# Loading the ninth query block of batch 0 behind the weights, and turning it between the first matmuls

## The chip, the cores and the metric

The kernel runs on one core of a Trainium2 chip. The metric is device time in microseconds (us) of one execution; the median over several executions is quoted. Positions inside an execution are from the profile and count from the start of the profiled span. Engines: PE is TensorE (matmuls), PEld its weight loads, DVE is VectorE, ACT is ScalarE, POOL is GpSimd.

## The reference, cut to what matters

```python
# q, k, v: (8 batches, 8 heads, 576, 64)
def phi(x, c, s):
    r = np.maximum(x, 0.0)
    return np.concatenate([r * c, r * s], axis=-1)      # c, s: cos and sin of the position
q_p, k_p = phi(q, cos_w, sin_w), phi(k, cos_w, sin_w)
kv  = einsum('bhsf,bhsd->bhfd', k_p, v)
num = einsum('bhsf,bhfd->bhsd', q_p, kv)
den = einsum('bhsf,bhf->bhs', q_p, k_p.sum(axis=2))[..., None] + 1e-06
attn = num / den
x = attn.transpose(0, 2, 1, 3).reshape(4608, 512)
h = x @ w_in                                            # 512 x 2048
g = h * (1.0 / (1.0 + np.exp(-beta * h)))
out = g @ w_out                                         # 2048 x 512
```

The linear attention is small beside the two matrix products. The kernel walks over x in chunks of 512 rows (8 blocks of 64). A batch has 576 rows, which are 9 blocks, so the ninth block of batch 0 is wanted only by chunk 1.

## The kernel before

The load of the inputs of one batch, and the order in which batch 0 starts:

```python
def load_raw(b, name, j0=0, j1=4):
    js = slice(j0, j1)
    src = {"q": q, "k": k, "v": v}[name][b]
    nc.sync.dma_start(
        out=raw_tile(b, name)[:, js].rearrange("q j n d -> q j (n d)"),
        in_=src.rearrange("(j g) (p n) d -> (g p) j (n d)", g=2, n=NQ)[:, js, :])
# ... cut ...
load_raw(0, "q", 0, 2)
load_raw(0, "q", 2, 4)
# ... cut: beta ...
load_raw(0, "v", 0, 2)
load_raw(0, "k", 0, 2)
load_raw(0, "v", 2, 4)        # what the start waits for
load_raw(0, "k", 2, 3)
load_raw(0, "k", 3, 4)
load_w("in", 0, 2)
# ... cut: later w_in 1, 2 and 3 ...
```

x is needed turned (features on partitions). Eight of the nine blocks of batch 0 are turned by TensorE, the ninth by a DMA that transposes. `q_relu` makes qb from the raw q, `q_turn_pe` turns qb into qt (and qs, its product with a tangent), `num_mm` multiplies these by kv, `x_rden` and `x_mul` divide. From here on TensorE works through slots: in chunk 0, slots 4 to 15 are four matmuls of h each, slots 16 to 31 four of the output each. What else is to be done hangs between slots:

```python
def rest():                                   # in slot 4
    cast_halves(2)                            # w_in 2 and 3 to bf16, mostly on VectorE
    cast_halves(3)
    x_mul(x_rden(2, 0, 8, NQ, (0, 1)), 8, NQ) # ninth block
    # ... cut: loads of w_out and of batch 1 ...
    x_turn_dma(0, 8, 9)                       # ninth block turned by a DMA
    for j in range(8):
        cast_out(j)                           # w_out to bf16, on VectorE
    v_scale(1, 0); k_relu(1); q_relu(1, 0); q_relu(1, 1)

early = {
    4: lambda: (num_mm(8, 0, 2, 0), num_mm(8, 1, 2, 1), rest()),
    15: lambda: v_scale(1, 1, eng="act"),
    22: lambda: (kv_mm(1, 0, 6), kv_mm(1, 1, 6), kv_take((0, 1), 6, "act")),
    23: second,                               # queries of batch 1 turned on TensorE
    25: lambda: (num_seven(0, 4), ...),       # 7 x 8 products of batch 1
    26: lambda: (num_seven(1, 6), ...),       # 7 x 8 more
    # ... cut ...
}
# in slot 24: load_raw(2, name) for q, v, k of batch 2
```

`warm_pe(n, w)` and `warm_long(n)` are matmuls whose results nobody uses; they fill TensorE's idle time at the start.

## Time and profile before

| | before |
|---|---|
| three runs | 294.04 to 295.37 us, median 294.3 |
| profiled span | 292.4 us |
| TensorE busy | 284.0 us (97%) |
| half of v lands | 12.40 us |
| VectorE's 20 casts of w_in end | 29.48 us |
| matmuls of kv of batch 1 begin | 38.08 us |
| first h of chunk 1 begins | 50.69 us |

How to read it: TensorE is the bound, so a change is worth what it moves TensorE's work.

### The profile page before, as it was taken

To read this page: it belongs to the slowest core of one execution; us is meant where nothing else is said; L and a number is where in the kernel's file an instruction comes from. 1 tells how busy PE (TensorE), PEld (TensorE's weight loads), DVE (VectorE), ACT (ScalarE), POOL (GpSimd) and SP (SyncE) were. 2 spreads that over 40 slices of the span, in tenths; PEclk is the share of its full clock that TensorE was granted. 3 is DMA by queue.
4 is the path that set the end of the run, shared out by engine and by line. 5 is a ranking of instruction groups with operands and counts; after the bars stand their busy time and mean duration, and the time that the engine had idled before them with its cause. 6 is when DMAs were issued, how large, how long until landed. Compare 5 with 4: busy or idle time off the path is not lost.

```text
span 292.4 us, 7218 instructions
## 1 busy us (share of the span) xinstructions
PE 284.0 (97%) x3072; PEld 141.3 (48%) x3072; DVE 114.0 (39%) x287; ACT 142.8 (49%) x228; POOL 74.9 (26%) x89
## 2 busy tenths in 40 slices
PE   7699999999999999999999999999999999999994
PEld 6354455455445544554445444454455444444444
DVE  5889975834900392029301950086005000000000
ACT  5778856862166315721573137412760277137511
POOL 1444000643380038202650265023601210000000
PEclk9999999999999999999999999999999999999999
DMA  6999999999998089907991699139102810131033
GB/s 242 383 389 385 392 349 334 299 264 336 176 284 314 3 159 203 402 34 141 216 392 46 130 217 391 58 65 206 36 2 52 143 36 0 39 83 23 0 74 72
DMA packets 50737, 53.89 MB, mean 184 GB/s; under 512 B 31233, under 2 KB 31633, under 8 KB 50705
## 3 DMA queue, kind: packets, MB, share of 16 engines
q1 hardware_dynamic: 47744, 45.95, 53.8%
q0 software_dynamic: 2688, 7.34, 10.5%
q8 instruction: 24, 0.39, 0.5%
q10 hardware_dynamic: 272, 0.14, 0.2%
q14 instruction: 9, 0.07, 0.1%
HBM read 36.71 MB, written 9.44 MB: 158 GB/s over the span
## 4 chain that ended last, share of the span: by engine, by line
PE 92%; DMA 3%; DVE 2%; SPq 1%; issue 1%
PE ps L365 42%; PE ps L390 42%; PE ps L280 3%; DMA raw_v<-in_v_dram 3%; PE ps L259 3%; PE ps L408 1%; SPq L78 1%; DVE xs L302 1%; PE ps L229 0%; PE ps L339 0%; DVE win L108 0%; DVE rden L295 0%; DVE den L291 0%; DVE rk L189 0%; DVE vb L204 0%
## 5 line engine op out<-in xcount | busy, mean ns | idle before, releaser
L365 PE MATMUL ps<-xt,win 128*128 128x512 bf16 (+1 forms) x580 | 127.3, 378 | 0.1
L390 PE MATMUL ps<-wout,g_t 128*128 128x512 bf16 x560 | 124.4, 379 | 0.0
L372 ACT ACTIVATE g_t<-ps,beta 128x512 bf16<-128x512 f32 x144 | 98.6, 688 | 33.2 <-PE ps L365 33.2
L365 PEld LDWEIGHTS <-win 128*128 128x128 bf16 x580 | 56.0, 98 | 66.0 <-issue 0.5
L390 PEld LDWEIGHTS <-g_t 128*128 128x128 bf16 x560 | 53.7, 98 | 63.9 <-issue 0.3
L385 POOL DMA_DIRECT2D out_dram<-o_sb x56 | 35.9, 645 | 136.7 <-ACT o_sb L396 136.7
L396 ACT COPY o_sb<-ps 128x512 f32<-128x512 f32 x35 | 20.2, 588 | 98.2 <-PE ps L390 94.0
L271 DVE CAST kv<-ps 128x520 bf16<-128x520 f32 x6 | 4.2, 700 | 68.3 <-PE ps L259 68.3
L217 POOL TENSOR_TENSOR qs<-qt,tanr 128x1152 bf16<-128x1152 bf16 x12 | 28.3, 2382 | 8.2 <-DMA qt<-qb 8.2
L411 DVE COPY o_sb<-ps 128x256 f32<-128x256 f32 (+1 forms) x2 | 0.7, 358 | 62.7 <-PE ps L408 62.7
L302 DVE TENSOR_TENSOR xs<-ps,rden 128x768 bf16<-128x768 f32 (+4 forms) x26 | 22.8, 884 | 0.9 <-DVE rden L295 0.2
L291 DVE TENSOR_TENSOR den<-ps,eps 128x12 f32<-128x12 f32 (+4 forms) x26 | 4.1, 159 | 33.6 <-PE ps L280 33.5
L214 DVE TENSOR_SCALAR vb<-raw_v,cos 128x256 bf16<-128x256 f32 x63 | 17.1, 347 | 0.0
L214 DVE TENSOR_SCALAR vb<-raw_v,sin 128x256 bf16<-128x256 f32 x54 | 14.7, 349 | 0.0
L280 PEld LDWEIGHTS <-qt 64*64 64x64 bf16 x576 | 10.4, 106 | 4.9 <-issue 4.5
L259 PE MATMUL ps<-vb,rk 64*64 64x130 bf16 x576 | 10.2, 218 | 2.1 <-ACT rk L187 1.9
L280 PE MATMUL ps<-kv,qt 64*64 64x65 bf16 x576 | 11.7, 195 | 0.5 <-ACT kv L269 0.5
L189 DVE TENSOR_SCALAR qb<-raw_q 128x1152 bf16<-128x1152 f32 x16 | 11.4, 752 | 1.6 <-DMA raw_q<-in_q_dram 1.6
L259 PEld LDWEIGHTS <-rk 64*64 64x64 bf16 x576 | 8.5, 106 | 6.9 <-ACT rk L187 3.6
L280 PE MATMUL ps<-kv,qs 64*64 64x65 bf16 x576 | 11.5, 193 | 0.0
L108 DVE CAST win<-w_stage 64x512 bf16<-64x512 f32 x22 | 10.9, 493 | 1.1 <-DMA w_stage<-in_moe_w_in_dram 0.6
L189 DVE TENSOR_SCALAR rk<-raw_k 128x2304 bf16<-128x2304 f32 (+2 forms) x9 | 10.7, 1186 | 0.6 <-DMA raw_k<-in_k_dram 0.6
(59 smaller groups left out, 98.6 us busy)
## 6 DMA issues: line engine op xcount, KB each, us to landing
raw_v<-in_v_dram SPq DMA_DIRECT2D x7, 1152.0 KB, 10.4
raw_k<-in_k_dram SPq DMA_DIRECT2D x7, 1152.0 KB, 13.6
raw_q<-in_q_dram SPq DMA_DIRECT2D x7, 1152.0 KB, 7.3
out_dram<-o_sb POOLq DMA_DIRECT2D x56, 128.0 KB, 4.4
w_stage<-in_moe_w_in_dram SPq DMA_DIRECT2D x3, 1024.0 KB, 13.4
w_stage<-in_moe_w_out_dram SPq DMA_DIRECT2D x2, 1024.0 KB, 8.0
w_stage<-in_moe_w_out_dram SPq DMA_DIRECT2D x4, 512.0 KB, 12.0
out_dram<-o_sb SPq DMA_DIRECT2D x14, 128.0 KB, 2.3
```

Source lines behind the costliest of these rows:

```text
L108: nc.vector.tensor_copy(o, a)
L189: nc.vector.tensor_scalar(dst, src, scalar1=0.0, scalar2=None, op0=ALU.max)
L214: nc.vector.tensor_scalar(o, a, scalar1=t[:, n : n + 1], scalar2=None, op0=ALU.mult)
L217: eng.tensor_tensor(dst.rearrange("q n (g p) -> q n g p", g=2), src.rearrange("q n (g p) -> q n g p", g=2), tanr[:, n0:n1].unsqueeze(2).to ...
L259: nc.tensor.matmul(t[jj * HP : (jj + 1) * HP, g], lhsT=rk[hs, n, 2 * jp + jj, :], rhs=vb[hs, n, 2 * jp + jj].rearrange("q s e -> q (s e)") ...
L280: nc.tensor.matmul(ps[cols, bank + jj, slot * E : (slot + 1) * E], lhsT=(qt, qs)[cs][rows, jp, n, cols], rhs=kv[rows, g, jp, cs, :], start ...
L302: nc.vector.tensor_tensor(o.rearrange("q j n s d -> q j (n s) d"), nv[:, :, a:z, :, 0:D].rearrange("q j n s d -> q j (n s) d"), rden[:, :, ...
L365: nc.tensor.matmul(ps[:, h_bank(c, jt), blocks.start * 64 : blocks.stop * 64], lhsT=win[jt // 4][:, mi, (jt % 4) * P : (jt % 4 + 1) * P], ...
L372: nc.scalar.activation(g_t, ps[:, h_bank(c, jt)], AF.Silu, scale=beta[:, jt : jt + 1])
L385: eng.dma_start(out=out_v[bb, n][:, m0:m1], in_=o_sb[hf * HP : (hf + 1) * HP, m0:m1])
L390: nc.tensor.matmul(o_ps, lhsT=gs[c, jt][:, tt * P : (tt + 1) * P], rhs=wout[jt // 4][:, jt % 4, :], start=(jt == 0), stop=(jt == JT - 1))
L396: nc.scalar.copy(o_sb, o_ps)
```

## The change

The intent: 131 KB less ahead of the loads that the start waits for. The ninth block of batch 0's queries is not wanted before chunk 1, so it is loaded behind w_in 3, and its relu, its turn, its products and its division move from the start to later slots.

```diff
-    load_raw(0, "q", 0, 2)
-    load_raw(0, "q", 2, 4)
+    load_raw(0, "q", 0, 2, 0, 8)          # load_raw takes blocks n0 to n1 now
+    load_raw(0, "q", 2, 4, 0, 8)
...
-    q_relu(0, 0)                          # and likewise q_relu(0, 1)
+    q_relu(0, 0, n1=8)
-    warm_pe(9, 48, bank=2)
-    q_turn_pe(0, 0, 4)                    # and likewise q_turn_pe(0, 1, ...)
+    warm_pe(11, 48, bank=2)
+    q_turn_pe(0, 0, 4, end=8)
...
     for i in range(1, 4):
         load_w("in", i)
+    load_raw(0, "q", 0, 4, 8, NQ)
...
+    def q_turn_eight(bank):               # two transposes on TensorE
+        t = ps[:, bank].bitcast(BF16)[:, 0 : 2 * P].rearrange("q (s c) -> q s c", c=P)
+        for jp in range(2):
+            nc.tensor.matmul(t[:, jp], lhsT=qb[:, jp, 8, :], rhs=ident,
+                             is_transpose=True, start=(jp == 0), stop=(jp == 1))
+        nc.scalar.copy(qt[:, :, 8], t)
+        for jp in range(2):
+            tan_mul(nc.vector, qs[:, jp, 8:NQ], t[:, jp].unsqueeze(1), 8, NQ)
...
     def rest():
         cast_halves(2)
         cast_halves(3)
-        x_mul(x_rden(2, 0, 8, NQ, (0, 1)), 8, NQ)
+        q_relu(0, 0, n0=8)
+        q_relu(0, 1, n0=8)
...
+    def eight():
+        for jp in range(2):
+            num_mm(8, jp, 2, jp)
+        x_mul(x_rden(2, 0, 8, NQ, (0, 1)), 8, NQ)
         x_turn_dma(0, 8, 9)
         for j in range(8):
             cast_out(j)
...
     early = {
-        4: lambda: (num_mm(8, 0, 2, 0), num_mm(8, 1, 2, 1), rest()),
+        4: rest,
+        11: lambda: q_turn_eight(1),
+        13: eight,
```

More of the change, by code (lines that the diff above doesn't have):

```diff
@@ L73, in raw_tile, with load_raw @@
         return raws[name, b]
-    def load_raw(b, name, j0=0, j1=4):
+    def load_raw(b, name, j0=0, j1=4, n0=0, n1=NQ):
         js = slice(j0, j1)
@@ L78, in load_raw @@
         nc.sync.dma_start(
-            out=raw_tile(b, name)[:, js].rearrange("q j n d -> q j (n d)"),
-            in_=src.rearrange("(j g) (p n) d -> (g p) j (n d)", g=2, n=NQ)[:, js, :])
+            out=raw_tile(b, name)[:, js, n0:n1].rearrange("q j n d -> q j (n d)"),
+            in_=src.rearrange("(j g) (p n) d -> (g p) j (n d)", g=2, n=NQ)[:, js, n0 * D : n1 * D])
     win = [const.tile([P, MI, 512], BF16, name=f"win{i}") for i in range(4)]
@@ L189, in relu, with q_relu @@
             nc.vector.tensor_scalar(dst, src, scalar1=0.0, scalar2=None, op0=ALU.max)
-    def q_relu(b, jp, eng="dve"):
-        relu(qb[:, jp].rearrange("q n (j d) -> q j n d", j=2), raw_tile(b, "q")[:, 2 * jp : 2 * jp + 2], eng)
+    def q_relu(b, jp, eng="dve", n0=0, n1=NQ):
+        relu(qb[:, jp, n0:n1].rearrange("q n (j d) -> q j n d", j=2),
+             raw_tile(b, "q")[:, 2 * jp : 2 * jp + 2, n0:n1], eng)
     def k_relu(b, j0=0, j1=4, eng="dve", n0=0, n1=NQ):
@@ L219, in tan_mul, with q_turn_pe @@
             tanr[:, n0:n1].unsqueeze(2).to_broadcast([P, n1 - n0, 2, HP]), op=ALU.mult)
-    def q_turn_pe(b, jp, bank, hold=False):
-        parts = ((0, 0, 5), (1, 5, NQ))
+    def q_turn_pe(b, jp, bank, hold=False, end=NQ):
+        parts = ((0, 0, 5), (1, 5, end))
         v2 = []
@@ L440 @@
     nc.vector.tensor_copy(ps[:, 0, 16 : 16 + NQ], sin9)
-    q_relu(0, 1)
+    q_relu(0, 1, n1=8)
     warm_pe(6, 128, bank=2)
-    warm_pe(9, 48, bank=2)
-    q_turn_pe(0, 0, 4)
+    warm_pe(11, 48, bank=2)
+    q_turn_pe(0, 0, 4, end=8)
     nc.vector.reciprocal(rbeta, beta)
     warm_pe(1)
-    take = q_turn_pe(0, 1, 2, hold=True)
+    take = q_turn_pe(0, 1, 2, hold=True, end=8)
     warm_long(2)
```

## The prediction

> **What bounds the kernel now.** I read the page first (busy shares, then the chain that ended last), then the chain in order of time for the first 60 us, then the timelines of PE, DVE, ACT, POOL and of the load queue for the first 55 us, and last the busy time in stretches. From the page:
>
> ```profile
> PE 284.0 (97%) x3072; PEld 141.3 (48%) x3072; DVE 114.0 (39%) x287; ACT 142.8 (49%) x228; POOL 74.9 (26%) x89
> PE 92%; DMA 3%; DVE 2%; SPq 1%; issue 1%
> ```
>
> TensorE is the bound: 92% of the chain is its work. The stretches show where it is not (columns: stretch, its length, then busy time and count of each engine, granted clock, DMA share, GB/s):
>
> ```profile
> 9.00:12.40 3.40, 1.53 (x83) 1.00 (x84) 2.64 (x3) 2.00 (x4) 1.63 (x1) 1.00 1.04 400
> 12.40:15.00 2.60, 1.85 (x63) 0.85 (x54) 2.50 (x7) 2.56 (x8) 1.26 (x1) 1.00 1.03 390
> 22.50:32.00 9.50, 9.50 (x46) 4.27 (x46) 9.10 (x21) 7.71 (x12) 2.50 (x4) 1.00 1.05 387
> 32.00:52.00 20.00, 19.97 (x318) 10.54 (x317) 14.01 (x30) 13.24 (x26) 1.02 (x2) 1.00 1.06 355
> ```
>
> From about 19 us to the end TensorE has no gap (9.50 of 9.50, 19.97 of 20.00; stretches from 52 to 280 us read 100% too). So only two things move the time: how early the gapless stretch begins, and whether something opens a gap in it. The start is set by loads; the chain in order of time (start, length, what) begins so:
>
> ```profile
> 3.06 9.34 DMA raw_v<-in_v_dram
> 12.42 0.35 DVE vb L204
> 14.74 1.06 DVE xs L302 x2
> 17.71 1.06 DVE xs L302 x2
> 18.82 0.40 PE ps L339 x4
> 19.22 3.03 PE ps L365 x18
> 22.25 0.25 PE ps L280 x16
> 22.50 9.60 PE ps L365 x44
> ```
>
> The second half of batch 0's v lands at 12.4 us; DVE, idle for 0.78 us before it, then works through to 18.77, and TensorE turns the last quarter of x and is dense from there. The last two lines matter for the gap: 0.25 us of the ninth block's products (slot 4), then 44 matmuls, four each for slots 5 to 15, 0.863 us a slot. DVE in the same time (start, length, instruction, idle before it):
>
> ```profile
> 19.33 10.16 DVE L108 CAST win<-w_stage 64x512 bf16<-64x512 f32 x20 [0.56 <-DMA w_stage<-in_moe_w_in_dram]
> 29.52 0.16 DVE L291 TENSOR_TENSOR den<-ps,eps 128x4 f32<-128x4 f32 x1
> 29.71 0.18 DVE L295 RECIPROCAL rden<-den 128x4 f32<-128x4 f32 x1
> 29.93 0.42 DVE L302 TENSOR_TENSOR xs<-ps,rden 128x256 bf16<-128x256 f32 x1
> 30.27 3.25 DVE L116 TENSOR_SCALAR wout<-w_stage,rbeta 128x512 bf16<-128x512 f32 x8
> 33.45 2.46 DVE L214 TENSOR_SCALAR vb<-raw_v,cos 128x256 bf16<-128x256 f32 x9
> 36.47 1.36 DVE L189 TENSOR_SCALAR rk<-raw_k 128x2304 bf16<-128x2304 f32 x1 [0.56 <-DMA raw_k<-in_k_dram]
> ```
>
> DVE casts w_in 1, 2 and 3 without a break from 19.33 to 29.48. Put beside TensorE's slots, this queue is only just ahead: the last cast for slot 12 (w_in 3, first half) ends near 28.15 and slot 12 begins at 22.44 + 7 x 0.863 = 28.48. That is the line the change touches.
>
> [...] The trace agrees on DVE: its rows stand in program order. [...] The trace agrees: the casts have median 422 ns and maximum 768, the long ones where POOL casts too (22.0 to 23.6 and 24.7 to 26.1 us). So the 20 casts take 10.16 us, not 20 x 0.44. [...] The new transfer has rows of 256 B; no load of before has such rows, so its price is not shown. [...] Before has idle of 1.40 us ahead of its first kv matmuls with a granted clock of 1.00.
>
> **The change, part by part.**
>
> Loads: the two q transfers shrink from 9 to 8 blocks: 128 x 4 x 256 B = 131 KB less ahead of everything that the start waits for. At 385 to 400 GB/s that is 0.34 us. v, k and w_in all land 0.34 earlier.
>
> Start, DVE and ACT: two relus, two tan products and two copies lose a ninth or a quarter of their width, two transposes leave, and two 48-wide warm matmuls come in to fill the place. DVE was idle 0.78 us before the v load, so this alone is worth nothing; it only makes sure DVE is ready for the earlier load. From there everything is a chain of DVE work and loads, so dense matmuls begin 0.34 earlier, at about 18.7 instead of 19.06. The casts of w_in 1 also wait for their load (0.56 us of idle), so they go from 18.99 to 29.14.
>
> Slot 4: the 16 small matmuls (0.25 us) go to slot 13; no work saved, but slot 5 now starts 0.34 + 0.25 = 0.59 earlier.
>
> Slot 11: two transposes, 0.05 us each of TensorE time, and they need qb of block 8. In DVE's order the two relus of it stand behind all 20 casts. One of them is 128 wide: from 1152 wide at 0.752 us and 2304 wide at 1.361, 0.53 ns per element, so 0.752 - 1024 x 0.00053 = 0.21 us; two back to back overlap by some 0.07, 0.35 together. They end at 29.18 + 0.35 = 29.53. TensorE has finished slot 11 at 28.48 - 0.59 = 27.89. It waits until about 29.42 for the first and 29.57 for the second: a new gap of 1.5 us. Slot 12 begins at about 29.65, against 28.48 before: 1.17 later, in spite of the earlier start. Both sides of this subtraction are on clocks that I have, so I trust it more than any other number here.
>
> Slot 13: ACT's copy and DVE's two tan products follow the transposes and end near 30.5, and slot 13 ends at 29.65 + 1.73 = 31.38, so its products don't wait; they cost the 0.25 that slot 4 gave up. TensorE is 1.42 late.
>
> w_out casts: they now stand behind the sums and division of slot 13. Products end at 31.63, sum, reciprocal and product take the 0.75 that they took before (29.52 to 30.27), so the casts start at 32.4 instead of 30.27, one each 0.406. The fourth is done at 34.1. Slot 16 starts at 31.94 + 1.42 = 33.36 and wants the fourth 0.65 later, at 34.0: some 0.1 us of wait. TensorE is now 1.5 late.
>
> Behind that: DVE ends these casts at 35.65, v at 38.1, relu of k at 39.45. The kv matmuls of batch 1 came at 38.08 and now at 39.6, so they just clear it. Nothing later has slack to give back.
>
> Sum: -0.34 (start) - 0.25 (slot 4 emptied) + 1.5 (gap) + 0.1 (transposes, nearly all of it after the gap) + 0.25 (slot 13) + 0.1 (first w_out casts) = about +1.4 to +1.5 us. 294.3 + 1.5 = 295.8.
>
> **Rivals.** A, no gap: the relus of block 8 come in time, and only the load counts: 294.3 - 0.34 + 0.1 = 294.0. For it: the slots look chosen with care, and the load lands in time. On the last point I estimate: w_in 3 is down at 24.7 in before (POOL waits for it until then), so at 24.4 now, and 131 KB at even half rate takes 0.7 us, so 25.1. Against it: the load is not the last thing waited for, the cast queue is, and its end at 29.48 stands in the profile; for no gap the casts would have to be 1.5 us faster. I give it 1 in 8. B, the gap also costs clock: [...] Against: idle of 1.40 us at 1.00. 1 in 25. C, the late DVE queue opens a second gap at the kv matmuls of batch 1: my margin there is 0.15 us, and the k load itself moves to 36.5 or 36.9 at its slow rate, still well ahead of the relu at 38.1. It would add 0.1 to 0.4: 296.1. 1 in 4. D, the narrower q gains more at the start than its bytes, because DVE and ACT there get shorter: up to 0.3 more, 295.5. The gap's far end moves with the casts' load, so such a gain survives only as far as w_in 1 lands earlier.
>
> **Range and chances.** The centre is the subtraction at slot 12 plus what follows, 295.8. The low end 294.7 holds a gap half as long as I think, the high end 296.6 rival C with some chip-to-chip spread (three runs of before span 1.3 us). A change of 2% would be 5.9 us, four times my effect: faster 0.005, same 0.985, slower 0.01.
>
> **What would show it.** The v load ends near 12.05 and TensorE's dense stretch starts near 18.7: the 0.34. DVE's row of 20 casts ends near 29.15, with two 128-wide relus behind it. TensorE's timeline shows two transposes near 29.5 with about 1.5 us of idle ahead of them, released by DVE's qb: if no idle stands there, the prediction is wrong. PE busy in 22.5 to 32 us falls from 9.50 to about 8. The w_out casts start near 32.4, slot 16 near 33.4, kv matmuls near 39.6. Granted clock stays at 1.00 behind the gap. What would make it wrong: casts that run faster than before, or a start that moves by much more than 0.34.

This is what the traces show. In before the rows of VectorE stand in program order (20 casts from 19.33 to 29.48 us, the sum at 29.52, the reciprocal at 29.71), and in after the two relus behind the same 20 casts began at 28.80, 0.03 us after the last cast's end. Of before's 20 casts, 16 took 418 to 424 ns and four 723 to 768, and those four overlapped GpSimd's casts (22.02 to 23.64 and 24.71 to 26.08 us).

## More of the kernel before

Instead of busy shares it is best to take landmarks, events on TensorE that both kernels have, and to compare their times; where the difference between the kernels jumps from one landmark to the next, something happened between them.

Chain of waits in order of time (start, length, what):

```profile
40.29 1.34 PE ps L229 x18
41.64 1.73 PE ps L390 x8
44.91 0.58 PE ps L280 x53
```

The 18 transposes of batch 1's queries took 1.34 us here, and after the change 1.00. The products of slot 26 (53 of the 56 in this line) follow without a gap.

## The result, and the profile after

| | before | after |
|---|---|---|
| fast runs | 6, median 294.44 us | 6, median 297.12 us (296.86 to 297.87) |
| ratio of the fast runs | | 1.009 (95%: 1.0068 to 1.0113) |
| profiled span | 292.4 us | 295.5 us |

All ratios here are the mean time of one kernel's fast runs over the mean time of the other's fast runs of the same rounds, so they are not quite the ratios of the medians. The change makes the kernel 2.7 us slower. That is within 2%, but above the range on record.

The page of the kernel after: busy times, then q8, the queue of kind "instruction" that has the most packets (packets, MB, share of 16 engines), then the chain that ended last.

```profile
PE 284.2 (96%) x3049; PEld 143.2 (48%) x3074; DVE 114.5 (39%) x291; ACT 142.6 (48%) x229; POOL 75.7 (26%) x89
q8 instruction: 24, 0.39, 0.5%
PE 88%; DVE 5%; DMA 3%; issue 2%; SPq 1%
```

TensorE's work is the same; its chain has lost 4 points, to DVE and to "issue", which is time in which an engine waits for nothing that the profile shows. The stretches, columns as in the prediction, say where (two of after, then the second one of before):

```profile
22.50:32.00 9.50, 8.70 (x56) 3.82 (x55) 7.32 (x20) 7.28 (x12) 2.00 (x3) 1.00 1.06 381
40.00:52.00 12.00, 10.20 (x220) 6.26 (x212) 8.00 (x16) 6.92 (x11) 0.00 (x0) 1.00 1.06 347
40.00:52.00 12.00, 11.97 (x215) 6.58 (x214) 8.22 (x16) 8.57 (x16) 1.02 (x2) 1.00 1.06 332
```

The first stretch lost 0.80 us of TensorE, which was foreseen in kind. The second lost 1.80 us (before was busy for 11.97 of those 12.00), which was not. VectorE's timeline shows the first cause (start, length, instruction, idle before it):

```profile
18.71 10.06 DVE L108 CAST win<-w_stage 64x512 bf16<-64x512 f32 x20
28.80 0.36 DVE L189 TENSOR_SCALAR qb<-raw_q 128x128 bf16<-128x128 f32 x2
32.23 3.25 DVE L116 TENSOR_SCALAR wout<-w_stage,rbeta 128x512 bf16<-128x512 f32 x8
```

The two relus do stand behind all 20 casts. TensorE's chain in order of time, at that place and at the second one:

```profile
29.08 0.36 PE ps L247 x2
29.45 1.73 PE ps L375 x8
...
45.89 0.15 PE ps L290 x4
46.05 1.54 issue
47.59 0.61 PE ps L290 x52
```

At 29.08 the two transposes begin, after 0.81 us of idle that DVE's qb ended. At 46.05, four products into the 56 of slot 26, TensorE stops for 1.54 us. No other engine, no semaphore and no data is named for it.

The landmarks on TensorE, from both timelines and chains:

| landmark | before | after | difference |
|---|---|---|---|
| dense h matmuls begin | 19.06 | 19.04 | -0.02 |
| slot 12 | 28.48 | 29.28 | +0.80 |
| slot 16 | 31.94 | 33.09 | +1.15 |
| kv matmuls of batch 1 | 38.08 | 39.43 | +1.35 |
| slot 24, behind the turned queries of batch 1 | 41.64 | 42.62 | +0.98 |
| first h of chunk 1 | 50.69 | 53.40 | +2.71 |
| first h of chunk 5 | 172.55 | 175.26 | +2.71 |

So two things make up the 2.7 us: about 1.0 us up to slot 24, and 1.54 us in the gap at 46.05. The small rest, 0.19 us, lies in pieces of a few hundredths. From chunk 1 to chunk 5 nothing more is lost. Near 194 us the chain of after has another 0.60 us of "issue", and this profiled execution has a total 0.4 us above what the medians differ by. It is not peculiar to after: TensorE's weight loads stand idle for 0.3 to 0.8 us at this place in 14 of the 20 profiles, in before's too (0.34 us, without a hole in its chain). It comes up again below.

**Why the earlier load gave nothing.** The second half of v lands at 11.98 instead of 12.40 us, and VectorE starts its next work earlier by as much. Two casts of w_in 0 then take it back. VectorE in before, then in after:

```profile
15.83 1.18 DVE L108 CAST win<-w_stage 64x512 bf16<-64x512 f32 x2
17.04 0.17 DVE L291 TENSOR_TENSOR den<-ps,eps 128x14 f32<-128x14 f32 x1
```

```profile
15.42 1.57 DVE L108 CAST win<-w_stage 64x512 bf16<-64x512 f32 x2
17.02 0.17 DVE L301 TENSOR_TENSOR den<-ps,eps 128x14 f32<-128x14 f32 x1
```

The pair starts 0.41 us earlier and takes 0.39 us longer (0.82 and 0.72 us each, against 0.42 and 0.72 in before). GpSimd casts other parts of w_in 0 at the same time: it starts them at 14.69 in after and at 15.30 in before, while VectorE starts at 15.42 and 15.83. That fits the long casts of before that the prediction reads (723 to 768 ns against 418 to 424, all four overlapping GpSimd's); the size of it is what the prediction lacked. Overlap alone does not make a cast long: the one at 15.83 in before took 0.42 us although GpSimd was casting (15.30 to 15.91 and 15.97 to 16.73). This is an argument from the two timelines, and the one experiment on it, below, did not settle it.

**What the second gap could be.** The page of after has on q8, of kind "instruction", 24 packets, 0.39 MB in all, which are 16 KB each, and TensorE's 3049 + 3074 records come to 255 for each packet. From these counts I took it that each packet brings TensorE a block of some 256 instructions (an estimate), and that TensorE stands idle if it gets to the end of one block before the next has come. Neither is shown by the counts alone. The DMA view of 1 us of each kernel (41 to 42 in before, 45 to 46 in after) shows the packet in question, first before, then after:

```profile
q1 hardware_dynamic: 200, 0.38, 103.7%
q8 instruction: 1, 0.02, 7.0%
```

```profile
q1 hardware_dynamic: 165, 0.38, 101.4%
q8 instruction: 1, 0.02, 7.0%
```

The engines are full of data packets in both, and 7.0% of 16 engines' microsecond is 1.1 us for this one packet in both (1112 ns by its own record, in both). What differs is when it starts. I counted this from the trace's single DMA records: 41.87 us in before, 45.05 in after, though TensorE reached the same place in its program only 1.0 us later. In after TensorE stopped behind its 612th weight load, 136 instructions or so past the 545th (numbers of weight loads in this document are places in the trace's row of weight loads, counted from 0, in which about ten semaphore waits and drains stand too; place 545 is the 535th to 537th load itself, depending on the kernel). The packet starts about when the 545th load does in before (0.26 us ahead of it) but 1.94 us behind it in after. The work goes on 2.54 us after the packet's start. This was the theory to test: *the gap at 46 is a late instruction packet*. Its rivals: the gap is a wait for data or a buffer that comes with the changed order; or the gap is a price of being late by any amount. And within the theory: what holds the packet back? In the expectations below, "fetch", "asked for" and "starves" are words of this theory: what is measured is the packet's start, and the time of asking is an estimate, the start of the 545th weight load. Near it stand the transposing DMA of x's ninth block (256 packets of 256 B, 42.36 to 44.51 us in after, 42.04 to 44.81 in before) and the loads of batch 2 that follow it.

### The profile page after: what moved, and what is told of

It is laid out like the page before. It is cut to its first block, busy times and chain, and to the rows that moved or that the text cites. A ratio compares the mean times of both kernels' runs of the same rounds, so it can differ in the third digit from the quotient of the medians.

```text
span 295.5 us, 7188 instructions
## 1 busy us (share of the span) xinstructions
PE 284.2 (96%) x3049; PEld 143.2 (48%) x3074; DVE 114.5 (39%) x291; ACT 142.6 (48%) x229; POOL 75.7 (26%) x89
## 4 chain that ended last, share of the span: by engine, by line
PE 88%; DVE 5%; DMA 3%; issue 2%; SPq 1%
PE ps L400 41%; PE ps L375 39%; DVE win L108 4%; PE ps L290 3%; DMA raw_v<-in_v_dram 3%; PE ps L269 3%; PE ps L418 1%; DVE xs L312 1%; SPq L78 1%; PE ps L230 0%; PE ps L349 0%; DVE rden L305 0%; DVE den L301 0%; DVE rk L189 0%; DVE vb L205 0%
## 5 line engine op out<-in xcount | busy, mean ns | idle before, releaser
L400 PE MATMUL ps<-wout,g_t 128*128 128x512 bf16 x535 | 120.7, 379 | 2.5 <-issue 1.6
L395 POOL DMA_DIRECT2D out_dram<-o_sb x56 | 36.8, 662 | 138.5 <-ACT o_sb L406 138.5
L189 DVE TENSOR_SCALAR qb<-raw_q 128x1152 bf16<-128x1152 f32 (+2 forms) x18 | 11.7, 686 | 0.3 <-DMA raw_q<-in_q_dram 0.3
L290 PEld LDWEIGHTS <-qs 64*64 64x64 bf16 x576 | 10.4, 105 | 1.6 <-issue 1.6
```

The source lines that it names most:

```text
L189: nc.vector.tensor_scalar(dst, src, scalar1=0.0, scalar2=None, op0=ALU.max)
L290: nc.tensor.matmul(ps[cols, bank + jj, slot * E : (slot + 1) * E], lhsT=(qt, qs)[cs][rows, jp, n, cols], rhs=kv[rows, g, jp, cs, :], start ...
L395: eng.dma_start(out=out_v[bb, n][:, m0:m1], in_=o_sb[hf * HP : (hf + 1) * HP, m0:m1])
L400: nc.tensor.matmul(o_ps, lhsT=gs[c, jt][:, tt * P : (tt + 1) * P], rhs=wout[jt // 4][:, jt % 4, :], start=(jt == 0), stop=(jt == JT - 1))
```

## The experiments

Before's median in the rounds of these runs was 294.26 to 294.51 us. All results were correct against the reference. Times are of fast runs.

### The relus between the casts

```diff
         cast_halves(2)
+        q_relu(0, 0, n0=8)
+        q_relu(0, 1, n0=8)
         cast_halves(3)
-        q_relu(0, 0, n0=8)
-        q_relu(0, 1, n0=8)
```

> The changed kernel with the two relus of block 8 moved on VectorE from behind the casts of w_in 3 to between those of w_in 2 and w_in 3. Theory 1 (two gaps, the second a consequence of the first: the relus make TensorE late at slot 11 by 0.8 us; being late, its next instruction fetch falls behind the DMA transpose of x's ninth block and starves it for 1.5 us near 46 us): both gaps go, TensorE is about as it was in the kernel before plus 0.1 us for two transposes in the dense stretch; 294.6 us, ratio to before 1.000 to 1.002. Rival 2 (the 1.5 us near 46 us belongs to the new instruction stream as such, not to its lateness): only the 0.8 us goes; 296.0 to 296.3, ratio 1.005 to 1.006.

Measured: 294.81 us (five runs, 294.78 to 295.26), ratio to before 1.0022 (1.0007 to 1.0037). That takes back 2.3 us of the change's 2.7. The chain:

```profile
28.34 0.11 PE ps L247 x2
28.46 1.73 PE ps L375 x8
...
45.43 0.08 issue
```

Both gaps are gone: the two transposes stand in the flow at 28.34, and 0.08 us is left of the 1.54. The instruction packet started at 42.26, with the 545th weight load. VectorE's timeline shows the moved relus, with six casts behind them:

```profile
25.95 0.66 DVE L189 TENSOR_SCALAR qb<-raw_q 128x128 bf16<-128x128 f32 x2
```

So the order of two small relus caused the first gap and, through the lateness it brought, the second. 0.81 + 1.54 = 2.35 us agrees with the gain. The earlier relu does not say what the second gap is.

### The ninth block turned on TensorE, no transposing DMA

```diff
-        x_turn_dma(0, 8, 9)
...
-        15: lambda: v_scale(1, 1, eng="act"),
+        15: lambda: (x_turn_pe(0, 8, 9, 0), v_scale(1, 1, eng="act")),
```

> The changed kernel with the ninth block of x turned by TensorE in slot 15 instead of by the DMA transpose; the late relus stay. Theory 1 (instruction fetch held behind the DMA transpose): the gap at slot 11 stays at 0.8 us, the 1.5 us near 46 us goes, two transposes cost 0.1; 295.6 to 295.9, ratio 1.004 to 1.005, and the 16 KB instruction packet is fetched near 42.9 us, not 45. Rival 2 (gap of the instruction stream itself, or of something other than the transpose): 297.0 to 297.3, ratio 1.009, gap still there.

Measured: 296.33 us (295.85 to 297.7), ratio 1.0076 (1.0052 to 1.01). The gap near 46 is gone:

```profile
45.79 0.97 PE ps L400 x4
46.76 0.71 PE ps L290 x52
```

The packet started at 44.22, 0.68 us behind the 545th weight load. The median fell by 0.8 us, not by 1.54, and lies above the 295.6 to 295.9 expected. For the profiled execution that is explained: v landed at 12.5 us and the transposes of slot 11 came at 29.95 instead of 29.08: 1.54 - 0.87 = 0.67 us, and its span is 0.7 us shorter than after's. For the other five runs it is not shown. Such differences between executions, half a microsecond and more in the landing of v, run through all that follows.

### Before, made late by dead matmuls

```diff
+        12: lambda: warm_long(1),        # 0.86 us; in the others (2), 1.72 us, and (4), 3.43 us
         15: lambda: v_scale(1, 1, eng="act"),
```

These three change nothing but TensorE's time. If lateness alone makes the gap, before must get it too.

> The kernel before with one pair of warm-up matmuls in fp32 (two passes, 1.12 us together in its trace) put into slot 12, so that TensorE is 1.1 us late and nothing else changes (four more rows in its program). Theory 1 (late, so the fetch meets the transpose): 1.1 less what the later load waits give back, plus a gap of about 1.5 us near 46 us; 296.6 to 297.2, ratio 1.008 to 1.009. Rival 2 (lateness itself costs nothing more): 295.2 to 295.6, ratio 1.003 to 1.004.

> The same with two pairs in slot 12, 2.2 us. Theory 1: the fetched instructions arrive when the transpose is over, at the same moment whether TensorE is 1.1 or 2.2 us late, so the gap shrinks by what the lateness grows: 296.7 to 297.3, within 0.3 us of the run with one pair. A rival in which the gap near 46 us is of a fixed length: 297.8 to 298.3. A rival with no gap: 296.3 to 296.6.

> The kernel before with four pairs of warm-up matmuls in slot 12 (a pair took 0.86 us in the runs with one and two, so 3.4 us late). The instruction packet would be asked for at about 45.2 us, when the DMA transpose of the ninth block, the same in all runs (42.0 to 44.9 us), is over. Theory 1, in the form that the run with two pairs left (a fetch asked for while the transpose is in the DMA engines starts some 2.2 us late and leaves a gap of 1.5 to 1.85 us; one asked for outside it does not): no such gap, 3.4 us and at most 0.3 of waits: 297.9 to 298.2, no more than the run with two pairs (298.0). Rival (any lateness costs a gap of that length): 299.6 to 300.0.

| | fast runs, us | ratio to before | gap near 46 | packet starts |
|---|---|---|---|---|
| before_late_1 | 294.86, 295.79, 297.06, 297.34 | 1.0066 (1.0037 to 1.0096) | 1.73 | 45.40 |
| before_late_2 | 297.58 to 298.95, median 298.03 | 1.0133 (1.0113 to 1.0152) | 1.85 | 46.26 |
| before_late_4 | 299.33 to 301.14, median 300.4 | 1.0186 (1.0135 to 1.0238) | 2.18 | 47.19 |

The profile of before_late_1 fell on a slow execution (299.41 us), so I take from it only the order of events; its four fast runs are of two kinds, about 2 us apart.

**A loss of clock behind the gap.** Four runs of the experiments were set aside as slow (299.41 and 299.65 us of before_late_1, one of late2_halves, one of early_order_halves). All four have a mean granted clock of 0.994. In the one with a profile, that of before_late_1, the trace's clock record stands at 0.50 from 48.98 to 52.40 us, right behind the gap of 1.73 us; one such window in 297.6 us makes the mean 0.994. That the gap brought it on is not shown: before_late_2's five runs and the six of after have their gap and clocks of 0.999 to 1.00. The fast runs, which are compared here, leave the loss out.

One line of the chain of before_late_2, and one of before_late_4:

```profile
46.99 1.85 issue
```

```profile
47.88 2.18 issue
```

Shown: the gap needs nothing of the change. A kernel that computes exactly what before does, 0.86 to 3.4 us later, gets it at the same weight load (the 613th). I had expected before_late_2 within 0.3 us of before_late_1, as if the gap only filled up the time to a fixed moment. It came later, by 1.6 us in the medians of fast runs, and still by 0.8 us against the slower two of before_late_1's fast runs, which is about the 0.86 us that was added: once open, the gap does not shrink when TensorE comes later. So the theory that the packet is late only while the transpose is in the DMA engines fell too: in before_late_4 the 545th load comes at 44.82, after the transpose has ended (44.6), and the packet still starts 2.37 us late. What is in the DMA engines by then are the loads of batch 2.

Why before has no gap of its own: its packet starts 0.17 us ahead of the transpose (41.87 against 42.04), relu_early's 0.05 us ahead of it. before_act's starts 0.08 us behind it and has no gap either, so the start of the transpose is at most roughly the edge, and it is not shown to be the cause. That before stands near an edge its own runs suggest: in the rounds of these experiments two of its executions took 297.24 us (clock 1.00) and 298.29 us (clock 0.994), against 293.6 to 295.3 for the rest. No profile of those was taken.

### One cast less on VectorE at the start

```diff
-    for gj, eng in zip(GJ, ("pool", "dve", "pool", "dve")):
+    for gj, eng in zip(GJ, ("pool", "dve", "pool", "act")):
```

> The kernel before with one of VectorE's two casts of w_in 0 given to ScalarE, which is idle then. Theory of the start (the casts of w_in 0, 0.72 to 0.82 us each on VectorE while POOL casts too and 0.42 when it doesn't, stand ahead of the last sums and divisions and decide when TensorE's dense stretch starts): one cast less, but the sums cannot start before TensorE's products end at 16.9 us, against 17.04 in the kernel before: 0.1 us earlier, 294.2 to 294.4, ratio 0.999 to 1.000. Rival (loads alone decide the start): no change, 294.4.

> The changed kernel with the relus between the casts of w_in 2 and 3 (as in the run before) and with one of VectorE's casts of w_in 0 given to ScalarE. In the changed kernel the products end at 16.48 us and the sums start at 17.02, so theory of the start: the dense stretch starts 0.45 to 0.5 us earlier, at 18.5 to 18.6 instead of 19.04; 294.3 to 294.5, against 294.8 for the early relus alone. Rival (loads, or the cast of w_in 1, decide the start): unchanged at 294.8.

Measured: before with it 294.13 us, ratio 0.9986 (0.9945 to 1.0027), two of six runs at 295.1 to 295.3; relu_early with it 294.96 us, 1.0015 (0.9963 to 1.0067). My expectation, dense matmuls 0.45 us earlier, missed. In relu_early with it VectorE's sums came at 16.93 instead of the 17.09 of relu_early, though v had landed 0.37 us later in this execution; but ScalarE's casts became the wait of TensorE (start, length, instruction, idle before it):

```profile
17.75 1.24 PE L375 MATMUL ps<-xt,win 128*128 128x512 bf16 x5 [0.36 <-ACT win L104]
```

The dense stretch began at 19.27, against 19.11 in relu_early. The theory that VectorE's slow cast takes the gain back is not refuted by this, but it isn't confirmed by an experiment either: at this place another engine is just as close behind.

### All mends together

relu_early and the cast on ScalarE, and the first four casts of w_out in slot 11, ahead of the sums of slot 13:

```diff
-        11: lambda: q_turn_eight(1),
+        11: lambda: (q_turn_eight(1), [cast_out(j) for j in range(4)]),
...
-        for j in range(8):
+        for j in range(4, 8):
             cast_out(j)
```

> The same and the first four casts of w_out put ahead of the sums and division of the ninth block, which took about 0.2 us of TensorE's time in slot 16 of the run with early relus. 294.1 to 294.3, ratio to before 0.999 to 1.000: if the load's 0.4 us counts at all, it shows here as at most 0.3 us.

Measured: 294.6 to 297.96 us, median 296.32, ratio 1.0047 (0.9997 to 1.0097). It missed: no better than relu_early, and spread over 3.4 us. The profiled execution was the slowest one: v landed at 13.25 us, all came later, the packet started at 45.83, and the gap was back with 2.10 us. So this kernel too falls on either side, from one execution to the next.

### What lies in the DMA engines: smaller loads, or no transpose, or later loads

The lateness of before_late_2 is kept, and one thing at a time is changed. First the loads of batch 2, which follow the transpose, in two halves each; second the ninth block turned on TensorE; third the loads moved behind batch 1's transposes (the total of that one means nothing, since batch 2 comes late; it was run for its profile, and run again).

```diff
 # late2_halves
             for name in "qvk":
-                load_raw(2, name)
+                load_raw(2, name, 0, 2)
+                load_raw(2, name, 2, 4)
 # late2_turn_pe: as in turn_on_pe, with warm_long(2) in slot 12
 # late2_loads_later, late2_loads_later_b (the same kernel)
-        if slot == 24:
-            for name in "qvk":
-                load_raw(2, name)
...
         x_turn_dma(1, 7, NQ)
+        for name in "qvk":
+            load_raw(2, name)
```

> The run with two pairs in slot 12 (1.72 us late, gap of 1.85 us, 298.0), but with q, v and k of batch 2 loaded in two transfers each instead of one; the DMA transpose of the ninth block stays. Packet theory (TensorE's instruction packet waits on its DMA engine for the share of one load that is being worked off there, 32 rows of 93 ns, 3 us, for a whole q, v or k, half of it for half a load): the fetch starts at most 1.5 us late, the gap shrinks to at most 0.6 us; 296.3 to 297.0. Transpose theory (it waits for the DMA transpose): unchanged, 297.8 to 298.3.

> The run with two pairs in slot 12, but the ninth block of x turned by TensorE in slot 15, no DMA transpose; the loads of batch 2 stay whole. Transpose theory: no gap, 1.72 us, 0.1 for the two transposes and up to 0.2 of waits: 296.3 to 296.6, all executions alike. Packet theory: between no gap and 1.9 us, by where the fetch falls in a load's share, so executions spread from 296.3 to 298.3.

> The kernel before with two pairs in slot 12, batch 2's q, v and k loaded behind the transposes of batch 1's last blocks instead of in front of them (near 55 us); they then come too late for batch 2's work, so the total says nothing and only the trace near 46 us is read. If the transpose alone holds the packet: still asked for near 43.4 us and at least 1.2 us late, until the transpose ends near 44.8. If the whole loads behind it are needed for it: the packet starts within 0.9 us of being asked for and no gap stands near 46 us.

> The same kernel as the run with batch 2's loads taken out of the time near 46 us, looked at a second time. If transpose and loads are both needed: again no gap near 46 us and the packet within 0.9 us of being asked for (43.0 to 44.3 us). If the first look was luck: a gap of 1 to 2 us.

The packet theory's 3 us is an estimate: a whole q, v or k is 512 rows of 2304 B, which over 16 engines are 32 each, at 93 ns a row (the median of before's 12288 packets of that size). That a packet waits for such a share was the guess.

| | fast runs, us | ratio to before | gap near 46 | packet starts |
|---|---|---|---|---|
| before_late_2, for comparison | median 298.03 | 1.0133 | 1.85 | 46.26 |
| late2_halves | 295.35 to 298.76, median 297.22 | 1.0097 (1.0062 to 1.0131) | none | 43.53 |
| late2_turn_pe | 295.63 to 297.07, median 296.38 | 1.0069 (1.0052 to 1.0086) | none | 43.29 |
| late2_loads_later | 311.55 (one look) | | none | 43.05 |
| late2_loads_later_b | 313.02 (one look) | | 0.92 | 43.62 |

Without the transpose the same lateness costs 1.65 us less (298.03 - 296.38, from two sets of rounds in which before had 294.43 and 294.38), and there is no gap. That is shown with times and with a profile. With halves the gap is gone in the profile, where the packet came in the middle of the transpose (42.19 to 45.01), but the runs are spread over 3.4 us, so it seems to help a part of the executions. With no loads behind the transpose the packet was not held back, in two looks, by more than 0.83 us; but in the second look, where I had expected no gap, the packet itself took 2.40 us instead of 1.1, and a gap of 0.92 us came of that. So something other than the whole loads of batch 2 can slow a packet; the transpose was in the DMA engines then (42.34 to 44.90), but that it was the cause is not shown, since in the first the packet took 1.10 us in the middle of it.

### The same halves, and the block turned on TensorE, on the kernels to be improved

before_halves is before with the halves alone. early_order_halves is relu_early with the w_out casts' order of the kernel above and the halves. early_order_pe is relu_early with that order and the ninth block turned on TensorE (the edits are those shown).

> The kernel before with q, v and k of batch 2 in two transfers each and nothing else. Both theories: the fetch comes in time in most executions as it is, so 294.2 to 294.5, ratio 0.998 to 1.000; by the packet theory also fewer executions near 295.3.

> The changed kernel with early relus, the first four casts of w_out ahead of the ninth block's sums, and batch 2's loads in halves: all gaps that I know of taken out. Packet theory: no execution with a gap near 46 us; 294.4 to 294.7, ratio 1.000 to 1.001 (two transposes in the dense stretch cost 0.1 us, and the earlier load is taken back by the casts of w_in 0). Transpose theory: as in the run before it with that order (294.6 to 298.0), a part of the executions still 1.5 to 2 us slower.

> The changed kernel with early relus, the first four casts of w_out ahead of the ninth block's sums, and the ninth block of x turned by TensorE, no padding. Theory 1: no gap at slot 11, none near 46 us in any execution; 0.2 us for four transposes in the dense stretch, the earlier load taken back by the casts of w_in 0: 294.4 to 294.8, ratio 1.000 to 1.002, executions within 1 us. Rival (something else in the changed kernel costs): above 295.2.

Measured: before_halves 294.34 us, 0.9998 (0.9982 to 1.0014); early_order_halves 294.66 to 297.86 us, median 295.23, 1.0056 (1.0022 to 1.0091); early_order_pe 294.59 to 296.8 us, median 295.31, 1.003 (0.999 to 1.007). Halves cost before nothing and give it nothing, as the theory has it where no packet is late (in before_halves it starts 0.18 us ahead of the 545th load). Neither of the other two beats before. early_order_pe has no gap near 46 in its profile (packet at 42.70, 0.40 us behind the 545th load). Both missed what was expected of them (at most 294.8 us, with executions close together); early_order_pe's median lies where its rival had put it, something else in the changed kernel that costs, and what that is stays open.

### The block boundary moved

If the gap is a block of instructions that runs out, more instructions ahead of it must move it to another place. One dead matmul in 32-bit at the start, which stands in before's trace as two matmuls (12.68 us, 1.12 us together), was replaced by 36 short ones, 34 weight loads more:

```diff
-    warm_long(1)
+    warm_pe(36, 48)
     kv_mm(0, 1, 6)
```

> The changed kernel with one pair of warm-up matmuls in fp32 near 13 us replaced by 36 small ones, in time in which TensorE has nothing to do: 34 more weight loads and matmuls ahead of everything that follows, so the packet is asked for during batch 1's kv matmuls near 40.5 us instead of 43. Packet late (theory 1): the gap near 46 us goes, that of 0.8 us at slot 11 stays; 295.4 to 295.8, 1.3 to 1.7 us less than the changed kernel, by adding instructions. Rival (the gap goes with the lateness of TensorE, whatever the packet): 297.0 to 297.3.

> The changed kernel with early relus, the first four casts of w_out ahead of the ninth block's sums, and the same padding; loads of batch 2 whole. Theory 1: both gaps gone in all executions; 294.3 to 294.7, all within 0.8 us of each other. Rival: as without the padding, a part of the executions 1.5 to 2.5 us slower (median above 295).

> The kernel before with two pairs in slot 12 (298.0 with a gap of 1.85 us) and the same padding. Theory 1: the lateness alone remains, 1.72 us and up to 0.2 of waits: 296.1 to 296.4. Rival: 297.8 to 298.3.

Measured: after with it 298.33 us (297.5 to 299.33), 1.0142; relu_early with the order of w_out casts and it 297.38 us (295.24 to 298.3), 1.0089; before_late_2 with it 298.93 us (297.53 to 301.07), 1.016. All three missed in time: I had expected after_pad at 295.4 to 295.8. But the gap near 46 is gone in all three profiles, as it should be, and a new one stands at the start. Weight loads of after_pad (start, length, instruction, idle before it):

```profile
18.49 0.13 PEld L290 LDWEIGHTS <-qs 64*64 64x64 bf16 x4
21.41 0.99 PEld L375 LDWEIGHTS <-win 128*128 128x128 bf16 x6 [2.79 <-issue]
```

A packet of that execution starts at 18.91, and 18.91 + 2.5 = 21.41, where TensorE goes on. The padding pushed another block's boundary into the densest part of the start, where 64 weight loads pass in 0.6 us (18.02 to 18.62). So the gap does move with the count of instructions, which no rival foretells, and moving it blindly costs about what it saves. In late2_pad the idle at that place was 3.58 us. The two gaps are 258 places of the row of loads apart (613 and 355), with as many matmuls 516 instructions, which is two blocks of 256 to within the count.

Part of these three times is clock, as after before_late_1's gap. A stretch of late2_pad (granted clock third from the end):

```profile
19.00:22.50 3.50, 2.33 (x6) 0.94 (x7) 3.31 (x8) 0.00 (x0) 0.37 (x1) 0.50 1.05 387
```

The clock records stand at 0.50 from 18.65 to 25.48 us in late2_pad and from 19.28 to 22.69 in early_order_pad, behind the gap, and from 12.65 to 16.06 in after_pad, ahead of it. Runs whose clock stayed at 1.00 took 297.5 us (after_pad), 296.58 and 295.24 (early_order_pad), 297.59 and 297.53 (late2_pad); these miss the expected times too. In after_pad's profile a further gap of 1.30 us stands at 227.12, and the packet before it starts 2.67 us ahead of its end.

### What all the profiles say of the packet

Counted from the single records of the traces: the start of TensorE's 545th weight load, the start of the packet, the difference, the gap at the 612th or 613th load, and the end of the gap less the packet's start (us).

| kernel | 545th load | packet | behind by | gap | goes on after |
|---|---|---|---|---|---|
| before | 42.12 | 41.87 | -0.26 | none | |
| before_halves | 41.65 | 41.48 | -0.18 | none | |
| relu_early_act | 42.65 | 42.55 | -0.11 | none | |
| relu_early | 42.28 | 42.26 | -0.02 | 0.08 | |
| before_act | 42.09 | 42.22 | 0.13 | none | |
| early_order_pe (no transpose) | 42.30 | 42.70 | 0.40 | none | |
| early_order_halves | 42.20 | 42.65 | 0.44 | none | |
| turn_on_pe (no transpose) | 43.54 | 44.22 | 0.68 | none | |
| late2_halves | 42.74 | 43.53 | 0.78 | none | |
| late2_turn_pe (no transpose) | 42.43 | 43.29 | 0.86 | none | |
| after | 43.11 | 45.05 | 1.94 | 1.54 | 2.54 |
| before_late_4 | 44.82 | 47.19 | 2.37 | 2.18 | 2.6 |
| before_late_1 (slow execution) | 42.80 | 45.40 | 2.59 | 1.73 | 2.50 |
| best | 43.14 | 45.83 | 2.69 | 2.10 | 2.57 |
| before_late_2 | 43.36 | 46.26 | 2.90 | 1.85 | 2.58 |

A gap of over 0.1 us stands exactly where the packet is 1.9 us or more behind (none was between 0.86 and 1.94), and TensorE always goes on 2.5 to 2.6 us after the packet's start. The second look at the later loads is the one exception, and there the packet took 2.40 us. This is the evidence that the gap is the packet.

A look at all 20 traces agrees. Take every idle stretch of over 0.5 us in the row of weight loads from 16 to 285 us that ends 2.3 to 2.8 us after the start of an instruction packet. They all stand at place 355, 613 or 614, 1384, 2410 or 2411, or 2795 of that row. These places are 258, 771, 1027 and 384 apart: 2, 6, 8 and 3 times 128 loads, which with their matmuls are 256 instructions, to within three. Place 2411 is the one near 194 us. In after its packet starts at 192.53 and TensorE goes on at 194.88, and no other DMA packet ran between 190 and 195 us: nothing in the DMA engines is needed for a gap of 0.6 us behind 138 small products.

All packets that were held back by 1.9 us or more near 46 us had the transpose of the ninth block and, behind it, the whole loads of batch 2.

**What stays open** is how the packet is held back. The DMA engines are full near the packet (103.7% and 101.4% of 16 engines in the two views above), so it may wait for other packets; this is a guess. It would not say why loads alone cost it 0.4 to 0.9 us, loads behind a transpose 1.9 to 2.9, and the transpose with nothing behind it 0.8 us in two looks. I have no run that tells the waiting in the queue from a slower engine.

## Why the prediction was wrong, by its own steps

- **Loads.** v was to land 0.34 us earlier and landed 0.42 us earlier. Right, in this execution; between executions of kernels with the same loads it varies by more than that (12.5 us in turn_on_pe, 13.25 in best). The 512 rows of 256 B, whose price the prediction could not read from before, took 18 ns each in after (median), where rows of 2304 B took 93: 0.57 of their bytes per ns; the prediction's "half rate" was an estimate.
- **"Dense matmuls begin 0.34 earlier."** Wrong: 19.04 against 19.06. The chain from the v load has a pair of casts in it that run beside GpSimd's, and the same pair took 1.57 us instead of 1.18. The prediction had seen that before's long casts (up to 768 ns, median 422) ran beside GpSimd's and did not ask whether an earlier start would change which of them overlap.
- **The 20 casts** were to end at 29.14 and ended at 28.77; they started at 18.71 and took 10.06 us.
- **The relus** took 0.36 us (0.35 foreseen).
- **The gap at slot 11.** The mechanism was right, released by DVE's qb and removed by relu_early, and the size was off: 0.81 us instead of 1.5. TensorE came later than foreseen by the 0.34 us that it did not gain, and the casts ended 0.37 us earlier. Slot 12 moved by 0.80 us, 1.17 foreseen.
- **w_out casts** start at 32.23, 32.4 foreseen. The kv matmuls moved by 1.35 us, 1.5 foreseen.
- **"Nothing later has slack to give back."** Wrong: by slot 24 the lateness is 0.98 us. Before had 0.34 us of wait in its turn of batch 1's queries (1.34 - 1.00): VectorE's relus there wait for the raw q, from 39.48 to 40.9 in before and from 39.41 to 40.8 in after, and TensorE in after comes only at 41.62.
- **The clock** behind the gap stayed at 1.00 in all six runs, as predicted, and rival B is out for this result. As a possibility it stays: in before_late_1's profile a gap of 1.73 us was followed by 3.41 us at a clock of 0.50. Rival A (no gap) is out too, and so is D (a gain at the start beyond the bytes): the start gained 0.02 us. Rival C, a second gap at the kv matmuls of batch 1, did not come as put: the kv matmuls moved by 1.35 us, less than the 1.5 that was foreseen without C.
- **The step that failed the total** is the search for what "opens a gap" in the gapless stretch. The sum has one gap, at slot 11, and the rivals one more, at the kv matmuls of batch 1; the 1.54 us at 46.05 is in neither. Up to slot 24 the sum came to 0.98 us instead of 1.5, so without the gap the time would have been about 297.12 - 1.54 = 295.6 us (an estimate), inside the range. The prediction compared engines and data; the instruction packets (here the one that started at 45.05 instead of 41.87), and what is in the DMA engines when one starts, were not looked at.

None of the 18 runs beats before by more than the noise: before with the ScalarE cast has 0.9986 (0.9945 to 1.0027), before with halves 0.9998 (0.9982 to 1.0014). The change's best form is relu_early, and it is 0.2% slower than before: its dense stretch starts no earlier (19.11 us), and its chain has 0.43 us of "issue" at 192.30, at the block boundary near 194 us named above, where before's has none.

## What to carry to other kernels

When work is moved into the shadow of a busy engine, read the engine's queue in program order and put the small operation that TensorE waits for ahead of the long ones: here two relus of 0.36 us moved ahead of six casts were worth 2.3 us. When a gap has no releaser, look at the instruction packets in the DMA view and count instructions to it; here 34 weight loads more at the start took it away from place 613 and put one at place 355, and it opened with 0.86 us of lateness (before_late_1), so a small measured difference can be such an edge and not the change. When a load lands earlier, follow the whole chain behind it, engine by engine: here v landed 0.42 us earlier and the dense matmuls began 0.02 us earlier.
